# Half of an elementwise product moved from GpSimd to VectorE, a small inverse moved the other way, and padded rows left out of the loads

## The chip, the cores and the metric

The kernel runs on one core of a Trainium2 chip: TensorE (PE) with its weight loads (PEld), VectorE (DVE), ScalarE (ACT), GpSimd (POOL), and SyncE (SP), which issues transfers. The metric is device time in microseconds, the median of several executions. One execution is also taken by the hardware profiler; its rows are quoted below, and L12 means line 12 of the kernel's file.

## The reference

A linear-attention block with decay (4 batches, 8 heads, 768 steps, 48 channels) feeds a mixture-of-experts block (3072 tokens of 384 channels, 8 experts, 1024 hidden).

```python
def _attn_ref(r, k, v, w, u):
    for t in range(S):
        cur = np.einsum('bhd,bhe->bhde', u[None] * kt, vt)
        y[:, :, t] = np.einsum('bhd,bhde->bhe', rt, state + cur)
        state = w[None, :, :, None] * state + np.einsum('bhd,bhe->bhde', kt, vt)
...
def _moe_ref(x, w_gate, w_local, w1, w2):
    # one expert a token: the previous token's where local_gate >= 0.5, else the argmax of the logits
            h = np.maximum(x[b, s] @ w1[e], 0.0)
            out[b, s] = p[e] * (h @ w2[e])
```

The change touches the attention block alone.

## The kernel before

The attention is done in 16 items: item n is a batch (n // 4) and a pair of heads (n % 4, called `hp`). A pair's 2 x 48 channels stand on the partitions 0 to 47 and 64 to 111; 48 to 63 and 112 to 127 hold zeros. The 768 steps are cut into 6 chunks of 128 (`NCH` = 6, `C2` = 3 of them are a half). Within a chunk, the state's decay is taken apart into powers of w. For each pair `tab[:, hp, 0]` holds the powers, `tab[:, hp, 1]` those of 1/w, both in SBUF; `inv` holds inverse powers made more exact, in PSUM. `mp` is a PSUM bank that lends room to `first` (the powers of the current pair, a copy that ScalarE makes), to `newton` and to `T` (the chunks' contributions to the state).

The program is written in the order in which each engine executes; nothing reorders it, and every engine works through its own list, waiting on semaphores. For one item the steps are:

- `load`: SP issues transfers of r and k (`rk`, 128 rows of 6144 bytes), of k and v by tokens (`kv`) and of v turned (`vT`). Four buffers of rk and vT, five of kv; loads run three items ahead.
- `scale`, on GpSimd: `ke` (keys times end powers), `pd` (r times k) and, from item 3 on, `rw` (r times powers), each in two instructions of three chunks.
- `keys`, on VectorE: `kw` (k times inverse powers); for items 0 to 2 also `rw`, with the powers read from `first`.
- `added` (TensorE, L249): ke times v into T. `states` (VectorE): a scan S over T.
- `scores` (TensorE, L291): kw against rw, two groups in two PSUM pairs that take turns (`banks`); VectorE then multiplies them by a mask into `am` (L293).
- `own` (TensorE, L268): pd summed into y; VectorE multiplies y by vT (L276).
- `inside` (L300, am and v into y) and `before` (L313, rw and S into y), both on TensorE, belong to the item before the current one; ScalarE copies y out (L321).
- `turn` (L332) transposes the result, `logits` (L345) and `token_logits` (L351) make the router's input once a batch.

`run` puts these in order. In iteration n TensorE does turn of n - 2, inside and before of n - 1, and from item 5 on the scores of n + 1, then own of n; `keys` runs two items ahead from item 6 on (`keys(n + 2)`, between y and the second mask of the scores), and `scale` one item ahead. For pair 1 the exact inverse is made in iteration 0 by `reciprocals(1)`, two VectorE instructions (L156, L157) that use `first` and `newton`; pairs 2 and 3 follow in iterations 1 and 3. `warm` gives TensorE transposes whose result nobody reads. `router.numbering` makes nine index tables on GpSimd, and `router.cast` turns six of them to float on ScalarE.

After the attention come ten groups of tokens through the experts; their code is the same before and after.

Of the kernel before, what the change touches and what calls it, by code (L numbers as in the profile page):

```python
# [11 lines left out]
F32 = mybir.dt.float32  # L12
I32 = mybir.dt.int32
Act = mybir.ActivationFunctionType
Alu = mybir.AluOpType
# [5 lines left out]
P = 128  # L21
B, H, S, DH = 4, 8, 768, 48
HP = H // 2
DP = 64
# [26 lines left out]
C2 = NCH // 2  # L51
AHEAD = 4
VB = NCH * 2 * DH


def spread(ap, axis, n):
# [5 lines left out]
class Attention:  # L62
# [13 lines left out]
    def __init__(self, tc, st, rk_d, kv_d, vT_d, x_d, w_t, wp_d, kept, ident, lt, mp):  # L76
        self.tc, self.nc = tc, tc.nc
        nc = tc.nc
        self.rk_d, self.kv_d, self.vT_d, self.x_d = rk_d, kv_d, vT_d, x_d
        self.w_t, self.kept, self.ident, self.lt = w_t, kept, ident, lt  # L80

        self.late = st.enter_context(tc.tile_pool(name="late", bufs=1))
        self.wp = self.late.tile([P, H, 32], F32, name="wp")
        self.inner = ExitStack()

        def pool(name, bufs, **kw):
            return self.inner.enter_context(tc.tile_pool(name=name, bufs=bufs, **kw))

        once = pool("once", 1)
        self.two = pool("two", 2)  # L90
        self.four = pool("four", 4)
        self.py = pool("py", 1, space=PSUM)
        ps = pool("ps", 1, space=PSUM)

        self.pairs = [ps.tile([P, 2, 512], F32, name=f"pair{i}") for i in range(2)]

        self.T = mp[:, 2 * P + 2:2 * P + 2 + (NCH - 1) * DH].rearrange("p (e c) -> p e c", c=NCH - 1)

        self.inv = pool("pinv", 1, space=PSUM).tile([P, HP, P], F32, name="inv")


        n = B * HP - 1
        self.rks, self.vTs = [None] * AHEAD, [None] * AHEAD
        for i in range(1, AHEAD + 1):
            self.rks[(n + i) % AHEAD] = once.tile([P, 2, NCH, P], F32, name=f"rk{i}")
        for i in range(1, AHEAD + 1):
            self.vTs[(n + i) % AHEAD] = once.tile([P, 2, C2, P], F32, name=f"vT{i}")
        self.kvs = [once.tile([P, 2 * VB + DP - DH], F32, name=f"kv{i}") for i in range(AHEAD + 1)]
        self.items = [dict() for _ in range(B * HP)]
        self.xTs, self.xs, self.lTs = {}, {}, {}  # L110
        for i in range(AHEAD - 1):
            self.load(i)
        nc.sync.dma_start(out=self.wp, in_=wp_d)


        self.step = once.tile([P, HP, DH, NCH - 1], F32, name="step")
        nc.vector.memset(self.step, 0.0)


        self.tab = tab = once.tile([P, HP, 2, P + 1], F32, name="tab")  # L120
        nc.vector.memset(tab[:, 0, :, 0:1], 1.0)
        nc.gpsimd.memset(tab[:, 1:, :, 0:1], 1.0)
        w = once.tile([P, HP, 2], F32, name="w")
        nc.vector.tensor_scalar(w[:, :, 0], w_t[:, :, 0], W_LO, W_HI, Alu.max, Alu.min)
        nc.vector.reciprocal(w[:, :, 1], w[:, :, 0])
        nc.vector.tensor_copy(tab[:, 0, :, 1], w[:, 0])
        nc.gpsimd.tensor_copy(tab[:, 1:, :, 1], w[:, 1:])
        n = 2
        while n <= P:
            m = min(n - 1, P + 1 - n)  # L130
            for engine, t in ((nc.vector, tab[:, :1]), (nc.gpsimd, tab[:, 1:])):
                engine.tensor_mul(t[..., n:n + m], t[..., 1:1 + m], t[..., n - 1:n].to_broadcast([P, t.shape[1], 2, m]))
            n += m

        self.first, self.newton = mp[:, :P + 1], mp[:, P + 1:2 * P + 1]
        nc.scalar.copy(self.first, tab[:, 0, 0])
        self.reciprocals(0)

        self.end = once.tile([P, HP, P + DP], F32, name="end")
        self.endT = once.tile([P, 2, HP, 2 * DH], F32, name="endT")  # L140
        self.align(26)
        self.warm(8)
        self.ends(slice(0, 1))
        self.turn_ends(slice(0, 1))
        self.warm(5)
# [7 lines left out]
    def reciprocals(self, i):  # L153

        nc, inv = self.nc, self.tab[:, i, 1, 1:]
        nc.vector.scalar_tensor_tensor(self.newton, self.first[:, 1:], -1.0, inv, Alu.mult, Alu.mult)  # L156
        nc.vector.scalar_tensor_tensor(self.inv[:, i], self.newton, 2.0, inv, Alu.add, Alu.mult)  # L157

    def warm(self, n):

# [28 lines left out]
    def load(self, n):  # L189
        nc = self.nc  # L190
        b, hp = divmod(n, HP)
        rk, vT, kv = self.rks[n % AHEAD], self.vTs[n % AHEAD], self.kvs[n % (AHEAD + 1)]
        if n:
            nc.sync.dma_start(out=rk.rearrange("p a c t -> p (a c t)"), in_=self.rk_d[b, hp])
        else:
            for z in (slice(0, C2), slice(C2, NCH)):
                nc.sync.dma_start(out=rk[:, :, z], in_=self.rk_d[b, hp].rearrange("p (a c t) -> p a c t", a=2, c=NCH)[:, :, z])
        nc.sync.dma_start(out=kv, in_=self.kv_d[b, hp])
        nc.sync.dma_start(out=vT.rearrange("p a c t -> p (a c t)"), in_=self.vT_d[b, hp])
        self.items[n].update(b=b, hp=hp, rT=rk[:, 0], kT=rk[:, 1], vT=vT,  # L200
                             k=kv[:, :VB].rearrange("p (c x) -> p c x", c=NCH), v=kv[:, VB:])

    def scale(self, n):

        nc, t = self.nc, self.items[n]
        t["ke"] = self.two.tile([P, NCH, 2 * DH], F32, name="ke")
        t["pd"] = self.two.tile([P, NCH, P], F32, name="pd")
        t["rw"] = self.four.tile([P, NCH, P], F32, name="rw")
        hp = t["hp"]

        def ke(p):
            z = slice(p, NCH if n == 0 else NCH - 1, 2)
            nc.gpsimd.tensor_mul(t["ke"][:, z], t["k"][:, z], spread(self.endT[:, p, hp], 1, len(range(NCH)[z])))  # L213

        def pd(i):
            z = slice(i * C2, (i + 1) * C2)
            nc.gpsimd.tensor_mul(t["pd"][:, z], t["rT"][:, z], t["kT"][:, z])  # L217

        def rw(i):
            self.decayed(nc.gpsimd, n, slice(i * C2, (i + 1) * C2))  # L220


        for what in (pd, ke) if n < 3 else (ke, rw, pd) if n == 4 else (rw, ke, pd):
            for i in range(2):
                what(i)

    def decayed(self, engine, n, z):
        t = self.items[n]
        pw = self.first[:, :P] if n < 3 else self.tab[:, t["hp"], 0, :P]
        engine.tensor_mul(t["rw"][:, z], t["rT"][:, z], spread(pw, 1, z.stop - z.start))  # L230

    def keys(self, n):
        nc, t = self.nc, self.items[n]
        t["kw"] = self.two.tile([P, NCH, P], F32, name="kw")
        inv = self.inv[:, t["hp"]]
        for z in (slice(0, NCH),) if n > 2 else (slice(0, C2), slice(C2, NCH)):
            nc.vector.tensor_mul(t["kw"][:, z], t["kT"][:, z], spread(inv, 1, z.stop - z.start))
            if n < 3:
                self.decayed(nc.vector, n, z)

    def added(self, n):

# [112 lines left out]
    def run(self, router, fetch, heads):  # L355
# [11 lines left out]
        for n in range(M + 1):  # L367
            if n + AHEAD - 1 < M:
                self.load(n + AHEAD - 1)
            if n == 0:  # L370
                self.scale(0)
                self.keys(0)
                self.tables()
                self.scores(0, 0)()
                self.scores(0, 1)()
                self.own(0)
                self.nc.scalar.copy(self.first, self.tab[:, 1, 0])
                self.turn_ends(slice(1, HP))
                self.warm(3)
                self.added(0)  # L380
                self.reciprocals(1)
                self.states(0)
                self.scale(1)
                continue
            if n < 3:

                self.keys(n)
                self.inside(n - 1)
                self.before(n - 1)
                if n == 2:  # L390
                    self.turn(0, pair("tp"))
                self.nc.scalar.copy(self.first, self.tab[:, n + 1, 0])
                self.scores(n, 0)()
                keep = self.scores(n, 1)
                keep()
                self.own(n)
                self.added(n)
                self.states(n)
                if n == 1:
                    self.reciprocals(2)  # L400
                else:
                    router.numbering()
                self.scale(n + 1)
                continue
            if n < M:
# [19 lines left out]
                router.slots(0)  # L425
            if n == M:
                router.shares(0)
            if n + 1 < M:
                self.scale(n + 1)
            if n == g + 6:  # L430
# [9 lines left out]
                router.same(0, 1)  # L440
            if M - 2 <= n < M:
                fetch(2 * (n - M + 2) + 1)
            if n == 6:
                router.cast()
            if n == M:
                break
# [1331 lines left out]
```

## Time and profile before

| | |
|---|---|
| median of 3 runs | 377.44 us (376.11 to 377.89) |
| profiled execution | 379.17 us, span 377.5 us, granted TensorE clock 0.996 |
| busy | PE 363.0, PEld 319.6, DVE 247.7, ACT 110.3, POOL 148.7 us |
| TensorE instructions of the attention | up to about 111 us of the span |
| moved by DMA | 74.93 MB, of these 64.79 MB read from HBM |

A row of the timeline gives start and duration in us, the engine, the line, the operation, what it writes and reads, its size and how many instructions were merged; in brackets stands the time that the engine was idle before it and what ended that wait. A row of the waits gives the waiting engine and line, what it waited for, the total in us, how often, and the longest.

### The profile page before, as it was taken

To read this page: it belongs to the slowest core of one execution; us is meant where nothing else is said; L and a number is where in the kernel's file an instruction comes from. 1 tells how busy PE (TensorE), PEld (TensorE's weight loads), DVE (VectorE), ACT (ScalarE), POOL (GpSimd) and SP (SyncE) were. 2 spreads that over 40 slices of the span, in tenths; PEclk is the share of its full clock that TensorE was granted. 3 is DMA by queue.
4 is the path that set the end of the run, shared out by engine and by line. 5 is a ranking of instruction groups with operands and counts; after the bars stand their busy time and mean duration, and the time that the engine had idled before them with its cause. 6 is when DMAs were issued, how large, how long until landed. Compare 5 with 4: busy or idle time off the path is not lost. (4 is left out here: it accounts for less than half of the span.)

```text
span 377.5 us, 9676 instructions
## 1 busy us (share of the span) xinstructions
PE 363.0 (96%) x3844; PEld 319.6 (85%) x3844; DVE 247.7 (66%) x718; ACT 110.3 (29%) x304; POOL 148.7 (39%) x207
## 2 busy tenths in 40 slices
PE   7899999999989999999999999999999999999992
PEld 6676777786769998999899999999999998989971
DVE  6988778888834835787557656857767767555300
ACT  4132233233532211322332233333243233331210
POOL 7689999786222055212333113313233023021012
PEclk9999999999999999999999999999999999999998
DMA  7999999983669457713352452164165065162011
GB/s 245 417 411 410 407 405 338 370 300 109 196 232 340 160 188 296 299 27 115 140 198 62 147 214 87 49 218 190 38 207 213 22 215 206 21 257 112 2 41 38
DMA packets 17765, 74.93 MB, mean 199 GB/s; under 512 B 2778, under 2 KB 6624, under 8 KB 15408
## 3 DMA queue, kind: packets, MB, share of 16 engines
q1 hardware_dynamic: 10336, 56.89, 40.7%
q0 software_dynamic: 3424, 9.48, 7.4%
q10 hardware_dynamic: 3952, 7.87, 5.7%
q8 instruction: 32, 0.52, 0.6%
q14 instruction: 21, 0.17, 0.1%
HBM read 64.79 MB, written 9.47 MB: 197 GB/s over the span
## 5 line engine op out<-in xcount | busy, mean ns | idle before, releaser
L1333 POOL DMA_INDIRECT out_dram<-yo,sid x27 | 26.6, 985 | 115.5 <-ACT yo L1328 92.0
L1184 PE MATMUL h<-exT,w1t 128*128 128x168 f32 (+4 forms) x240 | 54.9, 327 | 0.0
L1188 DVE TENSOR_TENSOR hT<-h,hs 128x168 f32<-128x168 f32 (+3 forms) x60 | 21.1, 351 | 46.1 <-PE h L1184 29.6
L1107 POOL DMA_INDIRECT xg<-x_d,gid x29 | 31.1, 1072 | 34.1 <-DVE gid L877 15.1
L1184 PEld LDWEIGHTS h<-exT,w1t 128*128 128x128 f32 x240 | 41.6, 190 | 0.3 <-issue 0.3
L1134 PE MATMUL h<-exT,w1t 128*128 128x168 f32 (+2 forms) x192 | 37.2, 333 | 0.5 <-DVE lt L698 0.5
L1253 PE MATMUL y<-factors,sums 128*128 128x192 f32 x168 | 36.8, 326 | 0.0
L293 DVE TENSOR_TENSOR am<-pair,kept 128x768 f32<-128x768 f32 x32 | 30.0, 953 | 8.9 <-PE pair L291 8.4
L217 POOL TENSOR_TENSOR pd<-rk 128x384 f32<-128x384 f32 x32 | 31.5, 1006 | 10.6 <-PE y L268 10.0
L1184 PE MATMUL h<-xs,ws 128*128 128x168 f32 (+4 forms) x144 | 35.3, 327 | 0.0
L1134 PEld LDWEIGHTS h<-exT,w1t 128*128 128x128 f32 x192 | 30.9, 190 | 2.6 <-DVE lt L698 0.6
L1184 PEld LDWEIGHTS h<-xs,ws 128*128 128x128 f32 x144 | 25.5, 190 | 4.3 <-ACT hs L1191 1.2
L1253 PEld LDWEIGHTS y<-factors,sums 128*128 128x128 f32 x168 | 28.9, 190 | 0.2
L291 PE MATMUL pair<-rw,kw 48*64 48x128 f32 (+1 forms) x768 | 23.4, 249 | 1.9 <-issue 1.1
L300 PE MATMUL y<-am,kv 128*64 128x128 f32 x360 | 22.9, 276 | 1.3 <-DVE y L276 1.2
L230 POOL TENSOR_TENSOR rw<-rk,tab 128x384 f32<-128x384 f32 x26 | 23.7, 936 | 0.4 <-DMA rk<-in_rk_dram 0.4
L1121 DVE COPY exT<-tp 128x384 f32<-128x384 f32 (+5 forms) x29 | 13.9, 485 | 14.7 <-PE tp L1120 14.6
L291 PEld LDWEIGHTS pair<-rw,kw 48*64 48x64 f32 x768 | 19.6, 133 | 4.6 <-issue 2.8
L1253 PE MATMUL y<-w2t,hT 128*128 128x192 f32 x96 | 23.0, 328 | 0.0
L213 POOL TENSOR_TENSOR ke<-kv,endT 128x288 f32<-128x288 f32 (+1 forms) x32 | 21.9, 705 | 1.9 <-DMA kv<-in_kv_dram 1.0
L321 ACT COPY xT<-y 128x768 f32<-128x768 f32 x15 | 12.0, 800 | 33.1 <-PE y L313 31.1
L300 PEld LDWEIGHTS y<-am,kv 128*64 128x64 f32 x360 | 19.4, 137 | 2.4 <-DVE y L276 1.7
(298 smaller groups left out, 736.6 us busy)
## 6 DMA issues: line engine op xcount, KB each, us to landing
w1t<-in_w_dram SPq DMA_DIRECT2D x8, 1536.0 KB, 6.9
w2t<-in_w_dram SPq DMA_DIRECT2D x8, 1536.0 KB
rk<-in_rk_dram SPq DMA_DIRECT2D x15, 768.0 KB, 8.4
kv<-in_kv_dram SPq DMA_DIRECT2D x16, 584.0 KB, 7.1
vT<-in_vT_dram SPq DMA_DIRECT2D x16, 384.0 KB
x_d<-x ACTq DMA_DIRECT2D x4, 1152.0 KB
w1t<-in_w_dram SPq DMA_DIRECT2D x2, 768.0 KB
w2t<-in_w_dram SPq DMA_DIRECT2D x2, 768.0 KB
```

The source lines that it names most:

```text
L213: nc.gpsimd.tensor_mul(t["ke"][:, z], t["k"][:, z], spread(self.endT[:, p, hp], 1, len(range(NCH)[z])))
L217: nc.gpsimd.tensor_mul(t["pd"][:, z], t["rT"][:, z], t["kT"][:, z])
L230: engine.tensor_mul(t["rw"][:, z], t["rT"][:, z], spread(pw, 1, z.stop - z.start))
L291: nc.tensor.matmul(sc[f * DP:(f + 1) * DP, h, i, x:], lhsT=t["kw"][q, c, o * DP:(o + 1) * DP], rhs=t["rw"][q, c, x:], start=True, stop=True)
L293: return lambda: nc.vector.tensor_mul(t["am"][:, g], sc, spread(self.kept[:, g:g + 3], 1, 2))
L300: nc.tensor.matmul(t["y"][h][p * DP:(p + 1) * DP, c2 * P:(c2 + 1) * P], lhsT=t["v"][:, (2 * c + h) * DH:(2 * c + h) * DH + DP], rhs=t["am" ...
L1107: self.nc.gpsimd.indirect_dma_start(out=xg[:n], out_offset=None, in_=self.x_d[:rows], in_offset=bass.IndirectOffsetOnAxis(ap=u["gid"][:n, ...
L1134: nc.tensor.matmul(h[:, :n], lhsT=u["w1"][:, m, kk, :], rhs=u["xT"][:, kk, :], start=(kk == 0), stop=(kk == DK - 1))
L1184: nc.tensor.matmul(out, lhsT=a, rhs=b, start=start and k == 0, stop=stop and k == len(terms) - 1, skip_group_check=True)
L1188: nc.vector.tensor_tensor(out, a, b, op=Alu.add)
L1253: return lambda: nc.tensor.matmul(bank[:, x * half:(x + 1) * half], lhsT=a, rhs=b, start=(j == 0 and x == 0), stop=(j == FK // 2 - 1), ski ...
L1333: self.nc.gpsimd.indirect_dma_start(out=out.rearrange("n (h d) -> (n h) d", h=2) if half else out, out_offset=bass.IndirectOffsetOnAxis(ap ...
```

## The change

- Pair 1's inverse powers are made by `inverse(1)`: three GpSimd operations on 128 x 128 elements into a new tile `more`, then a ScalarE copy into `inv`. The two VectorE instructions of `reciprocals(1)` go, and `warm(3)` in iteration 0.
- The second half of item 2's rw is made by GpSimd, ahead of its pd and ke, with the powers read from `tab`.
- The second half of rw of items 3 to 8 is made by VectorE in `keys`, after kw, with the powers read from `tab` in SBUF; GpSimd makes the first half.
- From item 4 on, rk and vT are loaded as two transfers of 48 rows each, without the rows of zeros (which the first four loads have left in the buffers). For item 4, kv is issued ahead of rk.
- `numbering` moves from iteration 2 to 8, `cast` from 6 to 8.

```diff
+SHARED = range(3, 9)
...
+    def inverse(self, i):
+        nc, w, inv = self.nc, self.tab[:, i, 0, 1:], self.tab[:, i, 1, 1:]
+        nc.gpsimd.tensor_mul(self.more, w, inv)
+        nc.gpsimd.tensor_scalar(self.more, self.more, -1.0, 2.0, Alu.mult, Alu.add)
+        nc.gpsimd.tensor_mul(self.more, self.more, inv)
+        nc.scalar.copy(self.inv[:, i], self.more)
...
-        if n:
-            nc.sync.dma_start(out=rk.rearrange("p a c t -> p (a c t)"), in_=self.rk_d[b, hp])
-        else:
-            for z in (slice(0, C2), slice(C2, NCH)):
-                nc.sync.dma_start(out=rk[:, :, z], in_=self.rk_d[b, hp].rearrange("p (a c t) -> p a c t", a=2, c=NCH)[:, :, z])
-        nc.sync.dma_start(out=kv, in_=self.kv_d[b, hp])
-        nc.sync.dma_start(out=vT.rearrange("p a c t -> p (a c t)"), in_=self.vT_d[b, hp])
+        rows = (slice(0, P),) if n < AHEAD else (slice(0, DH), slice(DP, DP + DH))
+        src = self.rk_d[b, hp].rearrange("p (a c t) -> p a c t", a=2, c=NCH)
+        if n == AHEAD:
+            nc.sync.dma_start(out=kv, in_=self.kv_d[b, hp])
+        for z in (slice(0, NCH),) if n else (slice(0, C2), slice(C2, NCH)):
+            for q in rows:
+                nc.sync.dma_start(out=rk[q, :, z], in_=src[q, :, z])
+        if n != AHEAD:
+            nc.sync.dma_start(out=kv, in_=self.kv_d[b, hp])
+        for q in rows:
+            nc.sync.dma_start(out=vT[q].rearrange("p a c t -> p (a c t)"), in_=self.vT_d[b, hp][q])
...
         def rw(i):
-            self.decayed(nc.gpsimd, n, slice(i * C2, (i + 1) * C2))
+            if i == 0 or n not in SHARED:
+                self.decayed(nc.gpsimd, n, slice(i * C2, (i + 1) * C2))
+        if n == 2:
+            rw(1)
...
     def decayed(self, engine, n, z):
-        pw = self.first[:, :P] if n < 3 else self.tab[:, t["hp"], 0, :P]
+        pw = self.first[:, :P] if n < 3 and engine is self.nc.vector else self.tab[:, t["hp"], 0, :P]
...
     def keys(self, n):
-            if n < 3:
+            if n < 2 or n == 2 and z.start == 0:
                 self.decayed(nc.vector, n, z)
+        if n in SHARED:
+            self.decayed(nc.vector, n, slice(C2, NCH))
...
     def run(self, router, fetch, heads):
                 self.turn_ends(slice(1, HP))
-                self.warm(3)
+                self.inverse(1)
                 self.added(0)
-                self.reciprocals(1)
                 self.states(0)
...
-                else:
-                    router.numbering()
...
+            if n == HP * 2:
+                router.numbering()
             if n + 1 < M:
                 self.scale(n + 1)
...
-            if n == 6:
+            if n == HP * 2:
                 router.cast()
```

Where the instructions stand: first VectorE from y of item 0 to the kw and rw of item 1, before:

```order
L276 TENSOR_TENSOR y<-y,vT_161 128x2x384
L156 SCALAR_TENSOR_TENSOR mp<-mp,tab 128x128
L157 SCALAR_TENSOR_TENSOR inv<-mp,tab 128x128
L255 SCALAR_TENSOR_TENSOR S<-step,mp 128x240
L237 TENSOR_TENSOR kw<-rk_158,inv 128x384
```

and after:

```order
L301 TENSOR_TENSOR y<-y,vT_161 128x2x384
L280 SCALAR_TENSOR_TENSOR S<-step,mp 128x240
L260 TENSOR_TENSOR kw<-rk_158,inv 128x384
L252 TENSOR_TENSOR rw<-rk_158,mp 128x384
L260 TENSOR_TENSOR kw<-rk_158,inv 128x384
```

GpSimd at the same time, from pd of item 0 to pd of item 1, after:

```order
L231 TENSOR_TENSOR pd<-rk_157 128x384 x2
L227 TENSOR_TENSOR ke<-kv_165,endT 128x3x96 x2
L164 TENSOR_TENSOR more<-tab 128x128
L165 TENSOR_SCALAR more<-more 128x128
L166 TENSOR_TENSOR more<-more,tab 128x128
L231 TENSOR_TENSOR pd<-rk_158 128x384 x2
```

The inverse has left VectorE's list and stands on GpSimd between items 0 and 1. The second place is VectorE in iterations 3 and 4, from kw of item 3 to am of item 4, before:

```order
L237 TENSOR_TENSOR kw<-rk_160,inv 128x768
L660 MEMSET r_ones 128x128
L255 SCALAR_TENSOR_TENSOR S<-step,mp 128x240
L293 TENSOR_TENSOR am<-pair_152,kept 128x768
L293 TENSOR_TENSOR am<-pair_151,kept 128x768
L276 TENSOR_TENSOR y<-y,vT_164 128x2x384
L237 TENSOR_TENSOR kw<-rk_157,inv 128x768
L255 SCALAR_TENSOR_TENSOR S<-step,mp 128x240
L237 TENSOR_TENSOR kw<-rk_158,inv 128x768
L293 TENSOR_TENSOR am<-pair_151,kept 128x768
```

and after:

```order
L260 TENSOR_TENSOR kw<-rk_160,inv 128x768
L252 TENSOR_TENSOR rw<-rk_160,tab 128x384
L684 MEMSET r_ones 128x128
L280 SCALAR_TENSOR_TENSOR S<-step,mp 128x240
L318 TENSOR_TENSOR am<-pair_151,kept 128x768
L318 TENSOR_TENSOR am<-pair_152,kept 128x768
L301 TENSOR_TENSOR y<-y,vT_164 128x2x384
L260 TENSOR_TENSOR kw<-rk_157,inv 128x768
L252 TENSOR_TENSOR rw<-rk_157,tab 128x384
L280 SCALAR_TENSOR_TENSOR S<-step,mp 128x240
L260 TENSOR_TENSOR kw<-rk_158,inv 128x768
L252 TENSOR_TENSOR rw<-rk_158,tab 128x384
```

A half of rw now follows each kw, ahead of S and of am. The third is VectorE in iteration 5, am of item 6, y of item 5, kw of item 7, second am and S of item 6, before:

```order
L293 TENSOR_TENSOR am<-pair_152,kept 128x768
L276 TENSOR_TENSOR y<-y,vT_162 128x2x384
L237 TENSOR_TENSOR kw<-rk_160,inv 128x768
L293 TENSOR_TENSOR am<-pair_151,kept 128x768
L255 SCALAR_TENSOR_TENSOR S<-step,mp 128x240
```

and after:

```order
L318 TENSOR_TENSOR am<-pair_151,kept 128x768
L301 TENSOR_TENSOR y<-y,vT_162 128x2x384
L260 TENSOR_TENSOR kw<-rk_160,inv 128x768
L252 TENSOR_TENSOR rw<-rk_160,tab 128x384
L318 TENSOR_TENSOR am<-pair_152,kept 128x768
L280 SCALAR_TENSOR_TENSOR S<-step,mp 128x240
```

The half of rw stands between kw and the second am; iteration 6 reads alike.

More of the change, by code (lines that the diff above doesn't have):

```diff
@@ L133, in __init__ @@
             n += m
+        self.more = once.tile([P, P], F32, name="more")
         self.first, self.newton = mp[:, :P + 1], mp[:, P + 1:2 * P + 1]
@@ L207, in scale @@
         t["pd"] = self.two.tile([P, NCH, P], F32, name="pd")
-        t["rw"] = self.four.tile([P, NCH, P], F32, name="rw")
+        self.room(n)
         hp = t["hp"]
@@ L225, in scale, with room @@
                 what(i)
+    def room(self, n):
+        t = self.items[n]
+        if "rw" not in t:
+            t["rw"] = self.four.tile([P, NCH, P], F32, name="rw")
     def decayed(self, engine, n, z):
         t = self.items[n]
-        pw = self.first[:, :P] if n < 3 else self.tab[:, t["hp"], 0, :P]
+        pw = self.first[:, :P] if n < 3 and engine is self.nc.vector else self.tab[:, t["hp"], 0, :P]
         engine.tensor_mul(t["rw"][:, z], t["rT"][:, z], spread(pw, 1, z.stop - z.start))
@@ L234, in keys @@
         t["kw"] = self.two.tile([P, NCH, P], F32, name="kw")
+        self.room(n)
         inv = self.inv[:, t["hp"]]
```

## The prediction

> **What bounds the kernel now.** I read the page's shares first, then the busy time of each engine from 14 to 45 us, the waits of TensorE and its weight loads up to 112 us, and then the timelines of TensorE (PE), VectorE (DVE) and GpSimd (POOL) up to 60 us, because every edit acts there. The lines are the page's first, one of the windows (PE, PEld, DVE, ACT, POOL, clock, DMA share), and two of the waits.
>
> ```profile
> PE 363.0 (96%) x3844; PEld 319.6 (85%) x3844; DVE 247.7 (66%) x718; ACT 110.3 (29%) x304; POOL 148.7 (39%) x207
> 14.00:45.00 31.00, 28.83 (x659) 21.35 (x651) 25.51 (x56) 7.64 (x16) 28.17 (x43) 1.00 1.02 410
> PE y L300 <- DVE y L276: 1.2, 2, 0.8
> PEld pair L291 <- issue: 2.8, 6, 1.1
> ```
>
> TensorE is busy 96% of the span. From 14 to 45 us GpSimd (28.17 of 31) and the DMA engines (share 1.02) are full, but neither is what TensorE waits for: its largest wait in the attention stage is 1.2 us for VectorE's y; its weight loads add 2.8 us of "issue" (a wait for nothing that the profile shows). What can be won or lost is therefore what the edits do to VectorE's chain from one item to the next, a few us at most.
>
> **Pair 1's inverse powers moved to GpSimd, three warm transposes dropped.** These are the rows of items 0 and 1, first TensorE, then VectorE, GpSimd and ScalarE.
>
> ```profile
> 10.87 0.49 PE L163 MATMUL pair<-ident 128*128 128x128 f32 x3
> 11.29 0.79 PE L249 MATMUL mp<-kv,ke 128*64 128x48 f32 x20
> 11.91 1.50 PE L300 MATMUL y<-am,kv 128*64 128x128 f32 x24
> 14.46 1.61 PE L291 MATMUL pair<-rw,kw 48*64 48x128 f32 x48
> 18.12 1.53 PE L300 MATMUL y<-am,kv 128*64 128x128 f32 x24 [0.82 <-DVE y L276]
> 20.42 0.80 PE L332 MATMUL pair<-ident,xT 112*128 112x112 f32 x6
> 10.64 0.96 DVE L276 TENSOR_TENSOR y<-y,vT 128x768 f32<-128x768 f32 x1
> 12.22 0.30 DVE L156 SCALAR_TENSOR_TENSOR mp<-mp,tab 128x128 f32<-128x128 f32 x1 [0.63 <-PE mp L249]
> 12.77 0.64 DVE L255 TENSOR_TENSOR_SCAN S<-step,mp 128x240 f32<-128x240 f32 x1
> 13.32 0.53 DVE L237 TENSOR_TENSOR kw<-rk,inv 128x384 f32<-128x384 f32 x1
> 14.70 0.55 DVE L230 TENSOR_TENSOR rw<-rk,mp 128x384 f32<-128x384 f32 x1
> 15.37 1.82 DVE L293 TENSOR_TENSOR am<-pair,kept 128x768 f32<-128x768 f32 x2
> 3.93 3.12 POOL L132 TENSOR_TENSOR tab<-tab 128x6 f32<-128x6 f32 x7
> 8.93 1.56 POOL L213 TENSOR_TENSOR ke<-kv,endT 128x288 f32<-128x288 f32 x2
> 10.89 1.97 POOL L217 TENSOR_TENSOR pd<-rk 128x384 f32<-128x384 f32 x2 [0.40 <-DMA rk<-in_rk_dram]
> 13.88 1.36 POOL L213 TENSOR_TENSOR ke<-kv,endT 128x288 f32<-128x288 f32 x2 [1.03 <-DMA kv<-in_kv_dram]
> 8.75 0.26 ACT L377 COPY mp<-tab 128x129 f32<-128x129 f32 x1
> ```
>
> Without the three transposes L249 starts at 10.87 instead of 11.29 and ends at 11.5. VectorE is free at 10.64 + 0.96 = 11.60, so the scan S starts there instead of at 12.77, and kw could start 0.55 later (13.32 - 12.77), at 12.15. It needs the new inverse: three dependent 128x128 operations on GpSimd after ke ends at 10.49. No row has that shape there; the table's seven dependent operations of 6 to 384 elements took 3.12 / 7 = 0.45 each, half a pd (384 elements) 1.0. I take 0.45, as most of those operations are shorter or about as short: 1.35 us, then ScalarE's copy at about 0.27 (0.26 for one column more): 12.1, just in time. At 1.0 it would be 13.8, and the gain below would be gone. GpSimd's delay is covered: pd of item 1 had to wait 0.40 for its load, and ke after it 1.03 for kv.
>
> TensorE: L300 of item 0 needs y (11.60), so it starts at 11.65, not 11.91. Then L300 and L313 take 2.30 (18.12 to 20.42): scores of item 1 start at 13.95 instead of 14.46. Their last rw now ends at 12.15 + (15.25 - 13.32) = 14.1, before the second group needs it. VectorE's am starts 0.91 after the scores, as in the rows, and am, am, y follow: L300 of item 1 starts at 17.6 instead of 18.12. **Gain 0.5**, kept as long as VectorE and TensorE hand on to each other; 0.65 if the scores' first group, not held at its start, is read as fast as in later items.
>
> **Item 2.** One half of rw leaves VectorE (0.55) and goes to GpSimd ahead of pd.
>
> ```profile
> 21.37 1.69 POOL L230 TENSOR_TENSOR rw<-rk,tab 128x384 f32<-128x384 f32 x2 [0.42 <-DMA rk<-in_rk_dram]
> 21.99 1.89 DVE L293 TENSOR_TENSOR am<-pair,kept 128x768 f32<-128x768 f32 x2 [0.72 <-PE pair L291]
> ```
>
> VectorE already waits 0.72 for TensorE there, so what it saves is worth nothing. GpSimd's extra half (1.0) pushes pd and ke of item 2, which are ready before own and added need them; the nine iotas leave just this place, and GpSimd waited 0.42 for rk behind them, so rw of item 3 starts when its load lands, as before. The iotas and the casts now stand at item 8, where GpSimd works an item ahead of TensorE: **0**. If GpSimd were late there, what shows is at most what it does now in their place.
>
> **The half of rw on VectorE, items 3 to 8.** GpSimd loses 0.85 to 1.0 per item, but nothing on TensorE waited for it: no gain. VectorE gains an operation of 384 elements whose second input is the table in SBUF; the older rw took its powers from PSUM (`mp`). That difference shows in other rows, first VectorE, then GpSimd at the same time:
>
> ```profile
> 71.81 0.89 DVE L709 SCALAR_TENSOR_TENSOR key<-lt,k 128x12 f32<-128x12 f32 x1
> 114.25 0.17 DVE L709 SCALAR_TENSOR_TENSOR key<-lt,k 128x12 f32<-128x12 f32 x1
> 97.21 0.55 DVE L813 TENSOR_TENSOR eqv<-si,ij_i 128x384 f32<-128x384 int32 x1
> 70.71 1.97 POOL L230 TENSOR_TENSOR rw<-rk,tab 128x384 f32<-128x384 f32 x2
> ```
>
> The same 12-element operation took 0.17 with GpSimd idle and 0.89 while GpSimd made rw, and it ended at 72.70, with GpSimd's second half (72.68). So an operation with two SBUF inputs waits for the GpSimd operation in flight. Alone, 384 elements cost 0.55 (97.21, GpSimd idle), or 0.47 in a row of others; on top comes a wait w between 0 and 1.0 (a whole half of rw or pd). Where it lands:
>
> ```profile
> 27.80 0.65 DVE L255 TENSOR_TENSOR_SCAN S<-step,mp 128x240 f32<-128x240 f32 x1 [0.70 <-PE mp L249]
> 34.66 1.82 DVE L293 TENSOR_TENSOR am<-pair,kept 128x768 f32<-128x768 f32 x2 [1.17 <-PE pair L291]
> 45.38 0.97 DVE L276 TENSOR_TENSOR y<-y,vT 128x768 f32<-128x768 f32 x1 [0.37 <-PE y L268]
> 47.12 0.95 DVE L293 TENSOR_TENSOR am<-pair,kept 128x768 f32<-128x768 f32 x1
> 48.43 0.28 PE L291 MATMUL pair<-rw,kw 48*64 48x128 f32 x2
> 52.44 0.95 DVE L293 TENSOR_TENSOR am<-pair,kept 128x768 f32<-128x768 f32 x1
> 53.89 0.27 PE L291 MATMUL pair<-rw,kw 48*64 48x128 f32 x2
> 56.16 0.97 DVE L276 TENSOR_TENSOR y<-y,vT 128x768 f32<-128x768 f32 x1 [0.44 <-PE y L268]
> 56.22 1.97 POOL L217 TENSOR_TENSOR pd<-rk 128x384 f32<-128x384 f32 x2 [0.55 <-PE y L268]
> ```
>
> - Item 3: ahead of S, which had 0.70 to spare: loss w - 0.23 (0.70 - 0.47), or 0.
> - Items 4 and 5: both ahead of am of item 4, which had 1.17 to spare: loss 2w - 0.23, or 0.
> - Item 6: the work on item 5's scores is long done; idle follows: 0.
> - Item 7: between y and the second am of item 6. That am ended at 48.07; the scores of item 7 reuse its bank and start at 48.43. With 0.05 for the semaphore, 0.31 to spare: loss 0.16 + w.
> - Item 8: the same place one item later; am ended at 53.39, the scores start at 53.89, so 0.45 to spare: loss 0.02 + w.
>
> For w: in items 7 and 8 GpSimd's pd is released by the same own as VectorE's y. Its two halves end 2.03 after y starts (58.19 against 56.16), while VectorE reaches rw 47.12 - 45.38 = 1.74 after: w about 0.28. In items 3 to 5 the phase is open; I take 0.28 there too, nearer to the lower end since GpSimd has less to do than before. Loss: 0.05 + 0.33 + 0.44 + 0.30 = **1.1** (w of 0: 0.2; w of 1.0: 4.7).
>
> [...]
>
> **96 rows from item 4.** Each item moves 1448 KB instead of 1736, but in five transfers instead of three.
>
> ```profile
> rk<-in_rk_dram SPq DMA_DIRECT2D x15, 768.0 KB, 8.4
> 57.58 0.38 SPq L194 DMA_DIRECT2D rk<-in_rk_dram  x1
> ```
>
> The load issued at 57.58 lands about 8.4 later, and items follow at 5.3 to 5.5 us; only 0.42 (21.37) was waited for a load after item 2, on GpSimd, and that load is unchanged. Two more issues per item cost SP 2 x 0.38. No row shows a 48-row transfer; between the same time per byte (each load earlier) and the time of a whole one for each half, nothing on TensorE moves until loads are over 2 us later. **0**.
>
> **Sum.** -0.5 + 0 + 1.1 + 0 = +0.6 on the profiled execution's 379.17, which lies 1.73 over the median of the runs (377.44). Forecast for the median: **378.0**.
>
> **Rivals.**
> - *VectorE's rw hardly waits.* If GpSimd, which now gets ahead and stands still for buffers, leaves gaps, w is near 0: loss 0.2, 377.44 - 0.3 = 377.1. For it: GpSimd's work falls by a fifth. Against: pd starts with y. Chance 0.25.
> - *The shared input decides: slower.* With w at 1.0 each time the loss is 4.7: 377.44 + 4.2 = 381.6. It takes over from w = 0.54, where the net is +1.9 (loss 0.31 + 0.85 + 0.70 + 0.56 = 2.4, less the 0.5). For it: GpSimd halves of 1.0 back to back. Against: met at a random phase, an operation of 1.0 has 0.5 left on average. Chance 0.15.
> - *Fewer bytes help TensorE's instruction supply: faster.* The waits put down to issue on L291's loads are 2.8 us in six pieces up to 112 us. If they shrink with the DMA load, 1.7 of them with w at 0 makes 375.4. Against, the longest one, in the timeline, and the window around it:
>
> ```profile
> 85.72 0.21 PE L291 MATMUL pair<-rw,kw 48*64 48x64 f32 x1 [0.84 <-issue]
> 80.00:90.00 10.00, 9.15 (x178) 6.46 (x174) 8.45 (x12) 2.22 (x5) 8.41 (x10) 1.00 0.35 130
> ```
>
> It falls where the DMA share was 0.35 already. Chance 0.09.
> - *Loads come late or the moved steps buy nothing:* the inverse at 13.8 removes the gain, 378.5. Chance 0.06, no change by measure.
>
> **How the numbers follow.** The forecast has 0.45. Half a per cent, 1.9 us, is about what a measurement of this kernel can tell from no change (the three runs span 1.8). Faster by more: 0.09. Slower by more: 0.15. Within: 0.45 + 0.25 + 0.06 = 0.76. The range goes from 376.2 (gain 0.65, w at 0, some issue time gone) to 379.7 (w near 0.6), leaving the ends of two rivals out.
>
> **What would show it.** L249 of item 0 near 10.9 and L300 of item 1 near 17.6; rw on VectorE at 0.55 to 1.5 each instead of 0.55, ending with GpSimd operations; S of item 3 and am of item 4 with less idle ahead of them; TensorE waiting for am ahead of the scores of item 7. I am wrong if those rw take 0.55 throughout, if the inverse comes after 12.5, or if TensorE's issue gaps change by over 1 us.

## The result, and the profile after

The changed kernel takes 395.22 us (median; the kernel before 377.65 beside it), 1.0445 times the time before, with a 95% interval of 1.0403 to 1.0486. The ratio leaves out two of the six runs (400.22 and 403.03 us), whose granted clock was lower (0.970 and 0.975 against 0.981), so it is smaller than the quotient of the medians. The forecast was 378.0, no change. The profiled execution took 395.18 us, its span is 393.5 us; before, the span was 377.5 us.

The loss lies in the attention. Here is TensorE's last transpose of the attention in the timelines, first before, then after:

```profile
110.34 0.45 PE L332 MATMUL y<-ident,end 112*128 112x112 f32 x3
```

```profile
127.16 0.45 PE L357 MATMUL y<-ident,end 112*128 112x112 f32 x3
```

The attention ends 16.8 us later, and the spans of the two profiled executions differ by 16.0: the whole loss is there. Next come the windows (TensorE, weight loads, VectorE, ScalarE, GpSimd, clock, DMA share, GB/s): from 25 to 50 us before, then after, with the two windows that the prediction showed.

```profile
25.00:50.00 25.00, 23.99 (x561) 18.48 (x562) 19.42 (x45) 6.59 (x18) 24.04 (x29) 1.00 1.03 409
```

```profile
25.00:50.00 25.00, 21.65 (x431) 16.02 (x426) 18.10 (x43) 4.28 (x8) 15.84 (x20) 0.86 1.03 233
```

```profile
14.00:45.00 31.00, 26.73 (x526) 19.61 (x520) 22.96 (x33) 6.14 (x15) 21.22 (x26) 0.89 1.03 281
80.00:90.00 10.00, 8.67 (x188) 6.71 (x186) 8.39 (x13) 2.30 (x6) 5.96 (x7) 1.00 0.75 219
```

The last two columns must be read together. The DMA engines are as busy as before (1.03) and move 233 GB/s instead of 409. In the trace's packets between 25 and 50 us the median row of 6144 bytes takes 420 ns instead of 238, and the kv rows between them, whose transfers are the same as before, 315 instead of 180. The transfers have become slow, not few. Who waits now: first the page's row of the 48-row transfers of rk (the last number is the median time in us from issue to landing, 8.4 for a whole rk before), then the waits between 15 and 127 us of GpSimd, VectorE and TensorE (total, times, longest), and last those of TensorE before:

```profile
rk<-in_rk_dram SPq DMA_DIRECT2D x24, 288.0 KB, 11.1
```

```profile
POOL rw L252 <- DMA rk<-in_rk_dram: 18.4, 12, 5.7
POOL ke L227 <- DMA kv<-in_kv_dram: 10.3, 10, 2.0
```

```profile
DVE kw L260 <- DMA rk<-in_rk_dram: 6.4, 3, 2.2
```

```profile
PE pair L316 <- issue: 5.3, 3, 2.9
PE pair L316 <- DVE am L318: 3.8, 3, 1.7
PE y L293 <- issue: 2.4, 3, 1.3
PE pair L357 <- DVE am L318: 1.0, 2, 0.6
PE y L325 <- DVE y L301: 0.7, 1, 0.7
```

```profile
PE y L300 <- DVE y L276: 1.2, 2, 0.8
PE pair L291 <- issue: 1.1, 2, 0.8
PE pair L332 <- DVE am L293: 0.3, 1, 0.3
```

GpSimd and VectorE stand for loads (before: 0.4 us in all), and TensorE for VectorE and for "issue" (nothing that the profile shows), 13.2 us in its five rows against 2.6 before. Of the 10.6 us on top, 6.6 are "issue", and none is put down to a load, so how the slow loads reach TensorE is shown only in part. The clock fell besides, to 0.86 from 25 to 50 us (1.00 before). This is TensorE's timeline around the longest gap:

```profile
26.90 0.45 PE L316 MATMUL pair<-rw,kw 48*64 48x128 f32 x9
30.27 1.65 PE L316 MATMUL pair<-rw,kw 48*64 48x128 f32 x38 [2.92 <-issue]
...
35.45 2.39 PE L325 MATMUL y<-am,kv 128*64 128x128 f32 x24
```

L325 takes 2.39 us where it took 1.53. The clock records have two stretches at half speed, 6.8 us from 30.5 and 3.4 us from 68.0, worth about 5.1 us of TensorE's work (half of the 10.2). They began 0.2 and 1.6 us after the two longest gaps had ended, of 2.92 us and, at 66.42, of 1.70; after the other gaps in the attention, all up to 1.52 us, there was none. Before there was none in the attention, and from 20 to 110 us the clock was 1.00 in the kernels below with 128 rows, with halves by columns and with 64 rows from partition 32. That the gaps brought the half clock is argued from this order. The extra waits (10.6) and the clock (5.1) give 15.7 of the 16.8 us.

### The profile page after: what moved, and what is told of

Its sections match the earlier page's. It is cut to its first block, busy times and chain, and to the rows that moved or that the text cites. A ratio compares the mean times of both kernels' runs of the same rounds, so it can differ in the third digit from the quotient of the medians.

```text
span 393.5 us, 9722 instructions
## 1 busy us (share of the span) xinstructions
PE 369.7 (94%) x3841; PEld 322.5 (82%) x3841; DVE 253.3 (64%) x721; ACT 110.6 (28%) x305; POOL 146.4 (37%) x205
## 5 line engine op out<-in xcount | busy, mean ns | idle before, releaser
L316 PE MATMUL pair<-rw,kw 48*64 48x128 f32 (+1 forms) x768 | 24.3, 255 | 9.5 <-issue 5.3
L316 PEld LDWEIGHTS pair<-rw,kw 48*64 48x64 f32 x768 | 20.4, 137 | 13.0 <-issue 6.6
L252 POOL TENSOR_TENSOR rw<-rk,tab 128x384 f32<-128x384 f32 x21 | 19.4, 937 | 18.8 <-DMA rk<-in_rk_dram 18.4
L325 PE MATMUL y<-am,kv 128*64 128x128 f32 x360 | 23.7, 283 | 0.7 <-DVE y L301 0.7
L325 PEld LDWEIGHTS y<-am,kv 128*64 128x64 f32 x360 | 20.3, 142 | 1.7 <-DVE y L301 1.1
```

Source lines behind the costliest of these rows:

```text
L316: nc.tensor.matmul(sc[f * DP:(f + 1) * DP, h, i, x:], lhsT=t["kw"][q, c, o * DP:(o + 1) * DP], rhs=t["rw"][q, c, x:], start=True, stop=True)
L325: nc.tensor.matmul(t["y"][h][p * DP:(p + 1) * DP, c2 * P:(c2 + 1) * P], lhsT=t["v"][:, (2 * c + h) * DH:(2 * c + h) * DH + DP], rhs=t["am" ...
```

## The experiments

Two theories of why 48-row transfers are slow were to be told apart, beside the one that the moved operations cost the time: the partitions that a transfer covers, or the number of transfers. What the expectations call the shared port is the wait in the prediction's rows, where VectorE's 12-element operation took 0.89 us instead of 0.17 while GpSimd made rw; no trace shows what is behind it. Ratios are to the kernel before, run beside each kernel.

**128 rows again, all else kept.**

```diff
-        rows = (slice(0, P),) if n < AHEAD else (slice(0, DH), slice(DP, DP + DH))
+        rows = (slice(0, P),) if n < AHEAD else (slice(0, P),)
```

> The changed kernel with all loads of 128 rows again, three transfers per item; everything else of the change stays (kv first for item 4 too). Half-array theory (a transfer that touches only partitions 0 to 47, or 64 to 111, moves about half the bytes per time, whatever its size): the loads run at 405 to 415 GB/s again, rw on GpSimd waits under 1 us for loads, 376.5 to 378.5 us. Transfer-count theory (five transfers instead of three are what costs): the same. Compute theory (the moved rw halves and the shared port are what costs): stays above 390.

Measured: 378.22 us, ratio 0.9974 (0.9944 to 1.0005). The window from 25 to 50 us:

```profile
25.00:50.00 25.00, 22.76 (x531) 17.15 (x530) 20.48 (x46) 5.78 (x11) 20.83 (x25) 1.00 1.03 410
```

The rate is back and so is the time. The other edits together have no effect that can be measured.

**Only the loads changed**, in the kernel before: `load` as in the changed kernel, nothing else.

> The kernel before with only the loads changed: two transfers of 48 rows for rk and for vT from item 4 on, kv first for item 4. Both load theories: the whole loss comes with this, 394 to 396 us, 225 to 245 GB/s between 25 and 50 us. Compute theory: 377 to 378.

Measured: ratio 1.0391 (1.0311 to 1.0470), and 232 GB/s from 25 to 50 us. The loss, 1.0445 with the whole change, is that of the loads.

**Two transfers of 64 rows, and two of half the columns.** Five transfers an item in both, with all bytes.

```diff
# halves by rows
+        rows = (slice(0, P),) if n < AHEAD else (slice(0, DP), slice(DP, P))
# halves by columns, from item 4 on
+            for a in range(2):
+                nc.sync.dma_start(out=rk[:, a], in_=src[:, a])
...
+        for a in (slice(0, 2),) if n < AHEAD else (slice(0, 1), slice(1, 2)):
+            nc.sync.dma_start(out=vT[:, a], in_=vsrc[:, a])
```

> The changed kernel with each rk and vT from item 4 on loaded as two transfers of 64 rows (partitions 0 to 63, then 64 to 127): five transfers per item as in the changed kernel, all 1736 KB as before. Half-array theory: still about half the bytes per time in rk and vT. If the price is per byte, an item's loads need about 7.2 us against 6.4 with 48 rows, so 12 items lose up to 10 us more: 400 to 406 us. [...] Transfer-count theory: as many transfers as in the changed kernel, so 393 to 397 us, with GB/s higher by a fifth.

> The changed kernel with each rk and vT from item 4 on loaded as two transfers of 128 rows and half the columns (r, then k; first half of vT, then second): five transfers per item as in the changed kernel, all 1736 KB as before. Half-array theory: every transfer touches all partitions, so 400 to 415 GB/s from 25 to 50 us and 376.5 to 379 us. Transfer-count theory: 393 to 397 us, at under 300 GB/s.

Measured: by rows 405.00 us, ratio 1.0682 (1.0636 to 1.0728); by columns 378.63 us, 1.0005 (0.9982 to 1.0028). The same window, by rows, then by columns:

```profile
25.00:50.00 25.00, 16.17 (x311) 11.58 (x309) 14.47 (x20) 3.48 (x7) 11.53 (x15) 0.80 1.02 209
```

```profile
25.00:50.00 25.00, 22.43 (x517) 16.87 (x517) 20.90 (x46) 5.26 (x11) 20.70 (x24) 1.00 1.04 399
```

Both have the same bytes and the same number of transfers; only the one whose transfers keep all partitions is fast. That settles the number of transfers: it costs 10 GB/s and no time that can be measured. The price by bytes held (400 to 406): 64 rows don't come for the price of 48 (395.22).

**One transfer of 112 rows.**

```diff
+        rows = (slice(0, P),) if n < AHEAD else (slice(0, U),)     # 0 to 111
```

> The changed kernel with one transfer of 112 rows (partitions 0 to 111) for rk and one for vT from item 4 on: three transfers per item, an eighth of the padded rows left out. Half-array theory: the first 64 rows and the other 48 are in flight together, so both halves of the array are reached, at 90 to 100% of the old rate in bytes per time: 377 to 379.5 us, 370 to 410 GB/s from 25 to 50 us, and no gain from the fewer bytes since no load was waited for. Rival (any transfer that isn't of all 128 rows is slow): 385 us or more, under 300 GB/s.

Measured: 396.42 us, ratio 1.0411 (1.0362 to 1.0459), against my theory.

```profile
25.00:50.00 25.00, 19.80 (x344) 14.90 (x339) 17.06 (x40) 3.48 (x7) 16.95 (x20) 0.78 1.02 258
```

It is not enough that both halves of the partitions are in the transfer. What was left is a guess, the map theory of the expectations below: which partitions a transfer covers decides its rate, and not how many. The 4.3, 5.8 and 7.2 us of loading an item in them are estimates from the runs above: 410 GB/s for kv and for a fast transfer (the rate with 128 rows), and half of it for a slow one, as two halves of 64 rows went at 209.

**Both halves from two queues.** Partitions 64 to 111 go by ScalarE's queue, 0 to 47 by SP's.

```diff
+                (nc.scalar if n >= AHEAD and q.start else nc.sync).dma_start(out=rk[q, :, z], in_=src[q, :, z])
```

> The changed kernel with its 48-row transfers, but those of partitions 64 to 111 issued by ScalarE's queue and those of 0 to 47 by SP's, so that both halves can be in flight side by side. If the two queues are served in turn, each half has its part of the array to itself at any time: 330 to 400 GB/s between 25 and 50 us and 377 to 381 us. Rival (two transfers to the two halves still go one behind the other, or ScalarE stands at its issues): 390 us or more, under 260 GB/s.

Measured: 402.41 us, ratio 1.0618 (1.0561 to 1.0676).

```profile
25.00:50.00 25.00, 20.64 (x368) 15.00 (x368) 15.55 (x21) 4.96 (x11) 13.84 (x17) 0.77 1.03 213
```

Side by side, as far as the two queues ran together, is no faster (213 GB/s against 233 from one queue). ScalarE besides stood for up to 10.5 us behind its load issues, which adds to the time (TensorE waited 3.8 us, in two waits, for one of its copies, L359).

**The partitions by themselves: 64 rows from partition 0, and 64 from partition 32.** The other 64 rows are left out. The count of rows, the bytes and the transfers are the same; only the partitions differ, and with them which 64 neighbouring rows of the source are read.

```diff
+        rows = (slice(0, P),) if n < AHEAD else (slice(0, DP),)     # one kernel
+        rows = (slice(0, P),) if n < AHEAD else (slice(32, 96),)    # the other
```

> The changed kernel, from item 4 on only with rows 0 to 63 of rk and vT (one transfer of 64 rows each; rows 64 to 127 are left out and stay as older items left them). The control for the kernel with rows 32 to 95. [...] Since an item then needs 4.3 us of loading, less than its 5.3 to 5.5 us of work, the time is 376 to 381 us. Any-count-but-128 theory: also slow per row.

> The changed kernel, from item 4 on only with rows 32 to 95 of rk and vT (one transfer of 64 rows each; the other rows are left out). As many rows, bytes and transfers as in the kernel with rows 0 to 63; only the partitions differ. [...] Any-count-but-128 theory, and a theory in which the source in HBM is what is slow: as slow per row as rows 0 to 63, about 430 to 480 ns.

Only the attention is read here: the later stages work on other values and took over 2 ms in both. The windows, each with the page's row of rk's transfers (the last number is the median time to landing), first partitions 0 to 63, then 32 to 95:

```profile
25.00:50.00 25.00, 18.29 (x300) 12.39 (x296) 13.17 (x18) 2.78 (x5) 14.16 (x17) 0.73 1.03 181
```

```profile
rk<-in_rk_dram SPq DMA_DIRECT2D x14, 384.0 KB, 8.4
```

```profile
25.00:50.00 25.00, 23.14 (x547) 17.55 (x545) 22.22 (x48) 5.78 (x11) 21.18 (x24) 1.00 0.80 285
```

```profile
rk<-in_rk_dram SPq DMA_DIRECT2D x14, 384.0 KB, 4.1
```

From partition 32 the DMA engines have idle time (0.80) at the higher rate, and from 20 to 50 us a packet of the loads' queue takes 165 ns in the mean (the queue's 70.5% of 16 engines' time, over 2051 packets), against 161 in the kernel with 128 rows; from partition 0 it takes 322. So it is not the count of rows, and hardly the source, which is the same tensor 32 rows further on: the partitions decide. How they do is not seen in the traces. I had expected 4.3 us of loading an item from partition 0, and no loss in time; it was worse, 181 GB/s, at which an item's 1160 KB take 6.6 us, and the attention ended at 124.2 us. From partition 32 it ended here:

```profile
109.59 0.45 PE L357 MATMUL y<-ident,end 112*128 112x112 f32 x3
```

That is 0.4 us ahead of the kernel with all 128 rows (110.00, below): even at full rate, leaving out half of rk and vT gives TensorE next to nothing.

**Three transfers: 32 to 95, 0 to 31, 96 to 127; and vT alone in 48 rows.**

```diff
+        rows = (slice(0, P),) if n < AHEAD else (slice(32, 96), slice(0, 32), slice(96, P))
# the other kernel: rk and kv as before
+        for q in rows if n < AHEAD else (slice(0, DH), slice(DP, DP + DH)):
             nc.sync.dma_start(out=vT[q].rearrange("p a c t -> p (a c t)"), in_=self.vT_d[b, hp][q])
```

> The changed kernel with each rk and vT from item 4 on in three transfers: rows 32 to 95, then 0 to 31, then 96 to 127; all bytes, seven transfers per item. Map theory: 64 rows at the full rate and two times 32 at half of it, an estimate of 5.8 us of loading per item (4.3 in one transfer, 7.2 as rows 0 to 63 and 64 to 127), about 310 GB/s while loads follow each other, and 379 to 388 us, far below the 405 of two 64-row halves. Any-count-but-128 theory: no transfer is fast, 403 to 410 us.

> The changed kernel with rk in one transfer of 128 rows again and only vT in two of 48 rows from item 4 on. Map theory: an estimate of 5.5 us of loading per item (6.6 with rk in halves too), about 305 GB/s while loads follow each other; that is about what an item's work takes (5.3 to 5.5 us), so little is lost: 377 to 384 us. If instead every slow transfer costs TensorE its own delay, vT has a third of the bytes of the slow loads: 5 to 7 us, 383 to 385 us.

Measured: three transfers 400.48 us, ratio 1.0587 (1.0513 to 1.0661); vT alone 386.39 us, 1.0213 (1.0140 to 1.0286). Windows in that order:

```profile
25.00:50.00 25.00, 22.41 (x475) 16.93 (x473) 19.70 (x45) 4.98 (x10) 14.68 (x17) 0.93 0.92 247
```

```profile
25.00:50.00 25.00, 20.67 (x436) 14.28 (x434) 18.16 (x43) 4.30 (x9) 16.85 (x20) 0.93 1.02 292
```

Both miss what I gave them. The three transfers reach 247 GB/s, more than two halves of 64 rows (209) and less than the estimate of 310; they lie between, but near the slow end. With vT alone no run shows the 5.5 us of loading (or the 6.6 with rk in halves too): 410 GB/s and half of it for vT would give 4.8. The rate came near the 305 all the same (292), but the time is above both expectations: at 292 GB/s an item's 1640 KB take 5.8 us, a little over the 5.3 to 5.5 between items, and that already costs 2.1%. Half of 410 GB/s for a slow transfer is thus too kind a picture, and I have no formula from GB/s to time.

**The other edits, with 128-row loads:** without the shared rw (`SHARED` empty), and with pair 1's inverse on VectorE and the warm transposes back.

```diff
-SHARED = range(3, 9)
+SHARED = ()
# the other kernel
-                self.inverse(1)
+                self.warm(3)
                 self.added(0)
+                self.reciprocals(1)
```

> 128-row loads, pair 1's inverse on GpSimd and item 2's half of rw as in the changed kernel, but all of rw of items 3 to 8 back on GpSimd. If VectorE's half with its wait for the shared port costs what the rows of the 128-row kernel show (turns of items 1 to 10 lose 1.9 us between 23 and 81 us), this is 1 to 2 us faster than that kernel: ratio to before 0.992 to 0.995, 375.5 to 377.5 us. If the loss is made up later, as at 86 us, where an issue wait of 0.84 us of the kernel before isn't seen: ratio 0.996 to 0.999.

> 128-row loads and the shared rw of items 3 to 8, but pair 1's inverse and the three warm transposes as in the kernel before. If the moved inverse is worth the 0.5 to 0.75 us that the rows of item 1 show, ratio to before 0.998 to 1.002, that is 0.5 to 1.5 us slower than with it (0.9974); if the gain is lost again in a later wait, the ratio stays at 0.996 to 0.998.

Measured: without the shared rw 377.84 us, ratio 0.9995 (0.9971 to 1.0018); without the moved inverse 377.63 us, 0.9988 (0.9968 to 1.0009). The end of the attention in the timelines of the 128-row kernel, of the one without shared rw, and of the one without the moved inverse:

```profile
110.00 0.45 PE L357 MATMUL y<-ident,end 112*128 112x112 f32 x3
```

```profile
109.14 0.45 PE L357 MATMUL y<-ident,end 112*128 112x112 f32 x3
```

```profile
109.64 0.45 PE L357 MATMUL y<-ident,end 112*128 112x112 f32 x3
```

The times don't tell the three apart; 0.9995 without the shared rw is above both ranges that I had given. In single traces, one of each kernel, the shared rw costs 0.86 us. The moved inverse brings turn of item 0 to 19.36 instead of 20.04, but at turn of item 4 both stand at 45.56: the 0.7 us is used up there.

## Why the prediction was wrong, point by point

**96 rows from item 4, priced at 0: the step that failed.** I put a 48-row transfer between "the same time per byte and the time of a whole one for each half", and took 0 "until loads are over 2 us later". The price lay inside these bounds: 420 ns a row against 238. The conclusion from it was wrong in two ways. First, I compared a delay of one load with a slack of 2 us, where a rate has to be compared with a pace. Before, an item's 1736 KB took 1,777,664 / 410,000 = 4.3 us, and items came at 5.3 to 5.5 us: room for a rate a fifth lower, not for half. Now an item's 1448 KB take 1,482,752 / 233,000 = 6.4 us, so each item adds about 1 us of delay. The slack is gone at item 4, the first with 48-row transfers: GpSimd waits for its kv and then for its rk, where before it waited for neither.

```profile
28.12 1.34 POOL L227 TENSOR_TENSOR ke<-kv,endT 128x288 f32<-128x288 f32 x2 [1.97 <-DMA kv<-in_kv_dram]
30.16 1.00 POOL L252 TENSOR_TENSOR rw<-rk,tab 128x384 f32<-128x384 f32 x1 [0.70 <-DMA rk<-in_rk_dram]
```

Second, I set a bound and did not carry it into the range: a rate of one half, which lay inside it, should have been a slower rival of its own. "Loads come late" stood among the rivals, but its price was only the gain that it would undo, 378.5.

**The rest of the sum, +0.6, was small, as it proved, but not confirmed.** With 128-row loads the kernel took 378.22 us, and the forecast for the whole was 378.0; that the two agree is luck, as the kernel before took 379.08 beside it. The ratio, 0.9974 (0.9944 to 1.0005), is -2.1 to +0.2 us, so the sum lies just above the interval.

- *Pair 1's inverse.* The signs came as announced, a little earlier. These are GpSimd, then TensorE, of the changed kernel; the prediction showed L300 at 18.12 and L249 at 11.29.

```profile
10.11 0.41 POOL L164 TENSOR_TENSOR more<-tab 128x128 f32<-128x128 f32 x1
10.61 0.29 POOL L165 TENSOR_SCALAR more<-more 128x128 f32<-128x128 f32 x1
10.99 0.46 POOL L166 TENSOR_TENSOR more<-more,tab 128x128 f32<-128x128 f32 x1
```

```profile
10.59 0.79 PE L274 MATMUL mp<-kv,ke 128*64 128x48 f32 x20
...
17.02 1.53 PE L325 MATMUL y<-am,kv 128*64 128x128 f32 x24 [0.70 <-DVE y L301]
```

  They took 0.41, 0.29 and 0.46 (0.45 each was taken). L325 of item 1 starts 1.1 earlier. Of this 0.37 is not the inverse's: the scores of item 0, ahead of it, already start at 7.49 instead of 7.86, and at 7.47 in the kernel without the moved inverse. That leaves 0.7 where I had 0.5. One reading was off on the way: L249, by its row, lasts 0.79 and not the 0.6 that I took, and VectorE's S of item 0 waited 0.27 for it. That the gain is kept is not so: it is gone at item 4.
- *rw on VectorE.* First and fourth of the six rows in the changed kernel:

```profile
26.10 0.55 DVE L252 TENSOR_TENSOR rw<-rk,tab 128x384 f32<-128x384 f32 x1
...
45.35 1.39 DVE L252 TENSOR_TENSOR rw<-rk,tab 128x384 f32<-128x384 f32 x1
```

  The wait is there: 0 to 0.84, mean 0.35 (0.28 was taken). In items 6 to 8 rw ended 0.41 after GpSimd's pd (46.74, 52.86 and 58.31, pd at 46.33, 52.45 and 57.90). With 128-row loads the six took 0.55 to 0.83, mean wait 0.10, a third of what I took; put item by item into the prediction's own sum, these waits give 0.5 where I had 1.1. The 0.86 of the traces lies between, and the times show no cost. That VectorE waits for GpSimd's operation was right; that the sizes lie so near is partly luck.
- *Instruction supply.* I had it as a gain of fewer bytes. It went the other way: "issue" waits on TensorE rose from 1.1 to 7.7 us, the sign that I had named as showing me wrong. From 15 us to the attention's end they were 0.7 to 1.7 in every kernel with full-rate loads, and 5 to 12 in those with slow ones, save the one with three transfers (2.1). A 16 KB instruction packet that started at 25.05 before starts at 27.48 in the changed kernel, 0.13 after the gap of 2.92 began, and takes 1.32 us instead of 1.10. That instructions queue behind the slow loads is argued from this; no run took it apart.

## What to carry to other kernels

Before loads are trimmed or split, ask which partitions each transfer covers: here 128 rows, or 64 rows from partition 32, went at full rate (161 and 165 ns a packet), and 48, 64 or 112 rows from partition 0 or 64 at 0.44 to 0.63 of its 410 GB/s, so that padding was cheaper to load than to skip. A DMA share of 1.0 with nobody waiting is not slack (1.03 here at 409 and at 233 GB/s); compare the bytes per item over the possible rate with the pace of the items, because a rate that falls below it makes a delay that grows (by about 1 us an item here). Where no load was waited for, fewer bytes gained next to nothing (0.4 us with half of rk and vT left out at the full rate), and any risk in the load is taken for that.

## What the runs showed of the hardware that I had not expected

With 112 rows in one transfer, on both halves of the partitions, the loads still went at 258 GB/s and not at 410, while with 64 rows from partition 32 a packet took 165 ns in the mean, about half of the 322 from partition 0. Where transfers were slow, so were the 128-row ones between them: kv rows took 315 ns instead of 180 in the changed kernel. And two gaps of TensorE cost twice, once as a wait and again as a half clock: after 2.92 and 1.70 us of idle time it lasted 6.8 and 3.4 us.
